# Attention and two gated layers on one core: block 0's softmax divided at its output

## The chip, the cores and the metric

One core of a Trainium2 chip runs the whole program. The metric is device time in microseconds (us). The engines are TensorE (PE in the profile; PEld is its weight load), VectorE (DVE), ScalarE (ACT), GpSimd (POOL) and SyncE (SP), which issues most DMAs.

## The reference

Attention over 2 batches, 8 heads, 768 positions and heads of 64, with a window of 96 positions and 8 global ones, then a SiLU layer (512 to 2048 to 512) and a gated sigmoid layer (512 to 1536 to 512) on the 1536 tokens. All is float32.

```python
def _attn_ref(q, k, v, n_global, n_local):
    scores = scale * np.matmul(q, k.transpose(0, 1, 3, 2))
    ...
    scores = np.where(keep, scores + bias, -1000000000.0)
    scores = scores - np.max(scores, axis=-1, keepdims=True)
    a = np.exp(scores)
    a = a / (np.sum(a, axis=-1, keepdims=True) + 1e-09)
    return np.matmul(a, v)

x = attention output, one row of 512 for each token
h = x @ w_in;  x = (h * sigmoid(h)) @ w_out
out = (sigmoid(x @ w_gate) * (x @ w_val)) @ w_out2
```

## The kernel before

Attention goes by 12 blocks of 128 queries (6 for each batch) and, in a block, by 4 pairs of heads p. One pair's steps: `emit_T` transposes the pair's q and k on TensorE into PSUM (two 128x128 products with an identity), ACT evacuates it for even pairs and DVE for odd ones into tile kt; `emit_QK` gives the scores of the two heads e in two banks; `scores` (in `soft`) adds the mask and takes the row's extreme on DVE (CUSTOM_DVE_ANT_0 in the profile, with a READ_ACCUMULATOR behind it); `exps` takes the exponential on ACT and sums each row with accum_out into ssum; `norm` adds 1e-9 to the sums, takes the reciprocal (128x2) and scales the exponentials, on DVE or POOL; `emit_PT` transposes them, ACT copies them to tile pt; `emit_PV` multiplies with v. After the fourth pair `take` splits the block's output into two parts of the two-part float format of the layers: ACT writes the high part of tile x, DVE the low part. A first block of a batch (i == 0, as block 0 is) has one key tile of 128, others two, so 128x256 scores.

Blocks 0 and 1 are run by `att_units` before anything else; from block 2 on `block_units` weaves the attention into the first layer's products (`macro`), until about 155 us; the rest is the two layers (`phase_rest`, `pair_loops`). Weights are loaded into stage tiles and converted on the way ("splits": one ACT copy to u, on DVE one TENSOR_SCALAR, two SCALAR_TENSOR_TENSOR and one TENSOR_TENSOR that writes w, all 128x512, and one more ACT copy).

Every instruction after `en.begin()` is recorded and then set in order by a planner (`order`), engine by engine, from the costs in `Op.cost` and the dependences that `link` finds. Each engine runs its own list in that order, so an instruction that comes late holds all behind it. In the planner's idle gaps on TensorE in the first blocks it sets filler products of a tile of zeros (warm). All recorded instructions carry one line (L269), so rows are told apart by tiles. In blocks 0 and 1 the transposes of q and k go to two banks in turn (bank 4, bank 6); later both halves of bank 4 are used. In its tail the kernel adds products to acc (`down`) and stores acc from SP.

Of the kernel before, what the change touches and what calls it, by code (L numbers as in the profile page):

```python
# [23 lines left out]
)  # L24
HA = 8
STORES = ((1, 3), (1, 2, 3), (0, 1, 2, 3))
SLOTS = sum(r[-1] for r in PLAN)
SLACK = 0.5
NEG = 1.0e30
# [89 lines left out]
class Issue:  # L119
# [22 lines left out]

    def link(self):
        last = self.last
        for i, o in enumerate(self.ops[self.first:], self.first):
            o.i = i
            for r, w in o.acc:
                if r[1] == bass.MemoryType.DRAM:
                    continue
                keep = []  # L150
                for j, rj, wj in last.get(r[0], ()):
                    hit = j != i and (w or wj) and meets(r, rj)
                    if hit:
                        o.pred.add(j)
                    inside = w and hit and r[2] <= rj[2] and r[3] >= rj[3] and len(r[4]) == 1 and all(
                        r[4][0][0] <= a and b <= r[4][0][1] for a, b in rj[4]
                    )
                    if not inside:
                        keep.append((j, rj, wj))
                keep.append((i, r, w))  # L160
                last[r[0]] = keep
        for o in self.ops[self.first:]:
            for j in o.pred:
                if j >= self.first:
                    o.left += 1
                    self.ops[j].succ.append(o.i)
# [134 lines left out]
def attn_moe_moe2_kernel(  # L301
# [14 lines left out]
    nc = tc.nc  # L316
# [20 lines left out]
    ident = const.tile([128, 128], F32, name="ident")  # L337
    nval = const.tile([128, 4], F32, name="nval")
    flag = const.tile([1, 1], I32, name="flag")
    X = [main.tile([128, 2, KD, G], F32R, name=f"x{g}") for g in range(NG)]  # L340
    acc = [main.tile([128, 4, 512], F32, name=f"acc{g}") for g in range(2)]
    nm_all = main.tile([128, NBLK, H], F32, name="nm_all")
# [26 lines left out]
    def defer(n, fn):  # L369
        seq[0] += 1  # L370
        deferred.append((clock[0] + n, seq[0], fn))
# [58 lines left out]
    def wtile(key):  # L430
        return W[slots[wid[key]]]
# [86 lines left out]
    def need_w(key):  # L518
        n = wid[key]
        while wst["split"] <= n:  # L520
            m = wst["split"]
            if m >= wst["dma"]:
                assert slot_free(m)
                dma_w(m)
                wst["dma"] = m + 1
            assert can_split(m)
            split_w(m)
            wst["split"] = m + 1
# [178 lines left out]
    def soft(n, sp, late=None):  # L707
        if sp is None:
            return
        gi, p = divmod(n, NP)  # L710
        s, i = gi % 2, gi % BLK
        w = 128 if i == 0 else 256
        t = next(t_r)
        t_t[n] = t
        c = 2.0 ** -(2 * p + 1)
        m0 = 0 if i == 0 else (128 if s == 0 else 256)
        ss = ssum[n % 4]

        def scores():
            for e in range(2):  # L720
                en.vector.tensor_tensor_reduce(
                    t[:, e, 0:w], sp[e], mask[e][:, m0:m0 + w], op0=ALU.add, op1=ALU.min,
                    scale=-c, scalar=3.0e38, accum_out=nm_all[:, gi, 2 * p + e:2 * p + e + 1],
                )

        def exps():
            for e in range(2):
                en.scalar.activation(
                    out=t[:, e, 0:w], in_=t[:, e, 0:w], func=AF.Exp, scale=-1.0,
                    bias=nm_all[:, gi, 2 * p + e:2 * p + e + 1], accum_out=ss[:, e:e + 1],  # L730
                )

        def norm():
            en.vector.tensor_scalar(ss, ss, 1.0e-9, None, op0=ALU.add)
            en.vector.reciprocal(ss, ss)
            for e in range(2):
                if n < 2 * NP and e == 0:
                    en.vector.tensor_scalar(t[:, e, 0:w], t[:, e, 0:w], ss[:, e:e + 1], None, op0=ALU.mult)
                else:
                    en.gpsimd.tensor_scalar(  # L740
                        t[:, e, 0:w], t[:, e, 0:w], ss[:, e:e + 1], 1.0, op0=ALU.mult, op1=ALU.mult
                    )

        if late:
            defer(late, scores)
        else:
            scores()
        d = n % 2 if late is None else late
        defer(1 + d, exps)
        defer(2 + d, norm)  # L750

    def emit_PT(n):
        gi, p = divmod(n, NP)
# [16 lines left out]
    def emit_PV(n):  # L770
        gi, p = divmod(n, NP)
        if n < 0 or gi >= NBLK:
            return
        s, i = gi % 2, gi % BLK
        pt = pt_t.pop(n)
        ps = bk["PV"][gi % len(bk["PV"])]
        if i == 0:
            vs = [v_t[gi]]
        else:
            vs = [v_t[gi], v_t[gi - 1]] if s == 0 else [v_t[gi - 1], v_t[gi]]  # L780
        nk = len(vs)
        for c in range(nk):
            for e in range(2):
                en.tensor.matmul(
                    ps[64 * e:64 * e + 64, p * 128:(p + 1) * 128],
                    vs[c][:, (2 * p + e) * D:(2 * p + e + 1) * D],
                    pt[:, (e * nk + c) * 128:(e * nk + c + 1) * 128],
                    start=(c == 0),
                    stop=(c == nk - 1),
                )  # L790

    def take(n):
        gi, p = divmod(n, NP)
        if n < 0 or gi >= NBLK or p < NP - 1:
            return
        i = gi % BLK
        ps = bk["PV"][gi % len(bk["PV"])]
        g, j = divmod(gi, BPG)
        xs = slice(j * 128, (j + 1) * 128)
        pv = ps.rearrange("p (a b) -> p a b", a=NP)  # L800
        en.scalar.activation(out=X[g][:, 0, :, xs], in_=pv, func=AF.Copy)
        en.vector.tensor_tensor(X[g][:, 1, :, xs], pv, X[g][:, 0, :, xs].bitcast(F32), ALU.subtract)
        if 0 < i < BLK - 1:
            en.sync.dma_start(
                out=v_t[gi][0:N_GLOB, :].rearrange("p (h d) -> p h d", h=H),
                in_=v[gi // BLK, :, 0:N_GLOB, :].rearrange("h p d -> p h d"),
            )
        load_v(gi + 2)
# [280 lines left out]
    def pair_loops(accs, evac):  # L1089
# [175 lines left out]

        def down(p, g, gts):
            keys = [("o2", 2 * p + j) for j in range(2)]
            end = p == C2 // 2 - 1
            stored = 0
            for t in range(4):  # L1270
                yb = bank[6 + ny[0] % 2]
                ny[0] += 1
                final = t == 3 and g == NG - 1
                runs = 2 if end and final else 1
                for h in range(runs):
                    cut = slice(h * 512 // runs, (h + 1) * 512 // runs)
                    for j, key in enumerate(keys):
                        need_w(key)
                        mm3_t(yb[:, cut], gts[g, j], slice(t * 128, (t + 1) * 128), wtile(key)[:, :, cut], j == 0, j == 1)
                        if final and h == runs - 1 and j == 1:  # L1280
                            done_w(keys[0])
                            done_w(keys[1])
                        yield unit()
                    a = accs[g][:, t, cut]
                    if p == 0:
                        en.scalar.activation(out=a, in_=yb, func=AF.Copy)
                    else:
                        en.vector.tensor_tensor(a, a, yb[:, cut], ALU.add)
                    if end and t in STORES[g]:
                        r0 = g * G  # L1290
                        en.sync.dma_start(
                            out=out[r0 + stored * 128:r0 + (t + 1) * 128, cut].rearrange("(t p) d -> p t d", p=128),
                            in_=accs[g][:, stored:t + 1, cut],
                        )
                if t in STORES[g]:
                    stored = t + 1

        def mm3_t(ps, gt, cols, w, first, last):
            with en.together():
                for i, (a, b) in enumerate(((0, 0), (0, 1), (1, 0))):  # L1300
                    en.tensor.matmul(ps, gt[:, a, cols], w[:, b, :], start=first and i == 0, stop=last and i == 2)
# [213 lines left out]

    with ExitStack():
        nc.vector.memset(warm, 0.0)
        make_identity(nc, ident)
        en.begin()
        load_qk(0)  # L1520
        make_iota()
        load_qk(1)
        load_v(0)
        load_v(1)
        make_n(qk_t.pop("n"))
        make_mask0()
        bk.update(SA=[bank[0]], SB=[bank[1]], PT=[bank[2], bank[7]], PV=[bank[3]], T=[bank[4], bank[6]])
        emit_T(0)
        emit_T(1)
        make_mask1()  # L1530
# [57 lines left out]
```

## Time and profile before

| | us |
|---|---|
| median of 3 runs | 637.54 (637.10 to 637.62) |
| the profiled execution | 636.38 |
| its span | 634.6 |
| TensorE busy, of the span | 622.5 |
| VectorE busy | 501.8 |
| ScalarE busy | 355.3 |
| GpSimd busy | 79.8 |

The busy times are averages over stages: VectorE's share is 79% of the span, and in the first 80 us far more. The groups below read the stages apart. TensorE's busy time includes modelled ends and fillers.

### The profile page before, as it was taken

How to read it: one execution, taken by the hardware profiler on the slowest of the kernel's cores; microseconds unless marked ns; L12 is line 12 of the kernel's file. 1: busy time of each engine (PE TensorE's matmuls, PEld its weight loads, DVE VectorE, ACT ScalarE, POOL GpSimd, SP SyncE). 2: the span in 40 equal slices, each digit the busy share in tenths (PEclk: the TensorE clock that was granted, in tenths of full speed). 3: DMA queues.
4: the chain of work that ended last, by engine and by line, in shares of the span. 5: the costliest groups of instructions: out<-in, count | busy, mean ns of one | idle time of the engine just before them, and what ended most of it. 6: DMA issues, size and time to landing. Idle time of an engine off the chain costs nothing.

```text
span 634.6 us, 9894 instructions
## 1 busy us (share of the span) xinstructions
PE 622.5 (98%) x3536; PEld 522.6 (82%) x3536; DVE 501.8 (79%) x1138; ACT 355.3 (56%) x751; POOL 79.8 (13%) x167
## 2 busy tenths in 40 slices
PE   8899999999999999999999999999999999999995
PEld 5589877888888888888888898898898898898894
DVE  6999995555379759698979998699789888986553
ACT  5898878655246456364546776754554553552430
POOL 5364445344110000000000000000000000000000
PEclk9899999999999999999999999999999999999999
DMA  8766652200012322222230102321412313200004
GB/s 235 194 163 181 180 135 52 52 19 2 1 34 67 94 72 67 66 68 84 83 100 1 37 31 77 124 66 35 126 40 68 101 33 93 86 22 1 0 35 170
DMA packets 65400, 49.07 MB, mean 77 GB/s; under 512 B 39616, under 2 KB 60352, under 8 KB 65344
## 3 DMA queue, kind: packets, MB, share of 16 engines
q1 hardware_dynamic: 64128, 48.11, 25.9%
q8 instruction: 29, 0.48, 0.3%
q10 hardware_dynamic: 1216, 0.26, 0.2%
q14 instruction: 27, 0.22, 0.1%
HBM read 45.22 MB, written 3.15 MB: 76 GB/s over the span
## 4 chain that ended last, share of the span: by engine, by line


## 5 line engine op out<-in xcount | busy, mean ns | idle before, releaser
L269 PE MATMUL bank<-x,w 128*128 128x512 f32 (+1 forms) x1104 | 238.0, 355 | 0.0
L269 PEld LDWEIGHTS bank<-x,w 128*128 128x128 f32 x1104 | 183.5, 189 | 27.9 <-issue 0.5
L269 PE MATMUL bank<-g,w 128*128 128x512 f32 (+1 forms) x624 | 145.5, 377 | 0.0
L269 PEld LDWEIGHTS bank<-g,w 128*128 128x128 f32 x624 | 110.6, 188 | 21.7 <-issue 0.7
L269 PE MATMUL bank<-w,g 128*128 128x512 f32 (+1 forms) x438 | 105.8, 387 | 0.0
L269 PEld LDWEIGHTS bank<-w,g 128*128 128x128 f32 x438 | 80.9, 188 | 16.7 <-issue 0.3
L269 DVE TENSOR_TENSOR acc<-acc,bank 128x512 f32<-128x512 f32 (+1 forms) x85 | 57.6, 678 | 32.7 <-PE bank L269 32.3
L269 ACT ACTIVATE m<-bank 128x512 f32<-128x512 f32 (+1 forms) x80 | 41.0, 516 | 68.3 <-PE bank L269 66.4
L269 PE MATMUL bank<-t,w 128*128 128x512 f32 x288 | 74.8, 390 | 0.0
L269 PEld LDWEIGHTS bank<-t,w 128*128 128x128 f32 x288 | 53.9, 188 | 11.5 <-ACT m L269 0.4
L269 DVE SCALAR_TENSOR_TENSOR u<-stage,u 128x512 int32<-128x512 int32 x84 | 58.5, 698 | 0.6
L269 DVE TENSOR_TENSOR m<-m,bank 128x512 f32<-128x512 f32 (+1 forms) x72 | 40.8, 574 | 18.3 <-ACT m L269 11.0
L269 ACT ACTIVATE w<-u 128x512 fp32r<-128x512 f32 x62 | 38.9, 627 | 26.6 <-DVE u L269 23.4
L269 ACT ACTIVATE t<-t,nm_all 128x256 f32<-128x256 f32 (+1 forms) x96 | 46.0, 481 | 9.9 <-DVE nm_all L269 9.4
L269 ACT ACTIVATE sg<-bank 128x512 f32<-128x512 f32 (+1 forms) x52 | 28.5, 548 | 39.5 <-PE bank L269 38.3
L269 POOL TENSOR_SCALAR t<-t,ssum 128x256 f32<-128x256 f32 (+1 forms) x88 | 44.8, 525 | 30.7 <-DVE ssum L269 17.8
L269 DVE TENSOR_TENSOR w<-u,w 128x512 fp32r<-128x512 f32 x62 | 43.2, 697 | 3.0 <-ACT w L269 2.7
L269 DVE SCALAR_TENSOR_TENSOR acc<-bank,acc 128x512 f32<-128x512 f32 x48 | 32.6, 689 | 10.0 <-PE bank L269 9.6
L269 DVE CUSTOM_DVE_ANT_0 t<-bank,mask 128x256 f32<-128x256 f32 (+1 forms) x96 | 34.7, 394 | 4.1 <-PE bank L269 2.7
L269 ACT ACTIVATE g<-sg 128x512 fp32r<-128x512 f32 x40 | 25.2, 630 | 21.8 <-DVE sg L269 12.5
L269 DVE SCALAR_TENSOR_TENSOR stage<-stage,stage 128x512 int32<-128x512 int32 x52 | 35.8, 688 | 0.2
L269 DVE TENSOR_TENSOR g<-m,g 128x512 fp32r<-128x512 f32 x44 | 30.0, 689 | 7.0 <-ACT g L269 6.6
(109 smaller groups left out, 718.7 us busy)
## 6 DMA issues: line engine op xcount, KB each, us to landing
stage<-in_moe_w_out_dram SPq DMA_DIRECT2D x28, 512.0 KB, 3.8
stage<-in_moe_w_in_dram SPq DMA_DIRECT2D x16, 512.0 KB, 3.8
stage<-in_moe_w_gate_dram SPq DMA_DIRECT2D x12, 512.0 KB, 3.4
stage<-in_moe_w_val_dram SPq DMA_DIRECT2D x12, 512.0 KB, 3.4
v<-in_v_dram SPq DMA_DIRECT2D x12, 256.0 KB, 2.9
qk<-in_k_dram SPq DMA_DIRECT2D x11, 256.0 KB, 3.1
qk<-in_q_dram SPq DMA_DIRECT2D x11, 256.0 KB, 4.1
out_dram<-acc SPq DMA_DIRECT2D x3, 512.0 KB, 2.7
```

The costliest lines, as they stand in the source:

```text
L269: getattr(getattr(self.nc, o.eng), o.meth)(*o.args, **o.kw)
```

## The change

For block 0 alone (LATE_SUMS = 1) the exponentials stay undivided and lose accum_out, and `norm` is left out. Behind the products with v the same transposed exponentials are multiplied with a tile of ones into a bank of their own, SUM (bank 6), so that each output row has its sum beside it. In `take` VectorE adds 1e-9 to that bank (128x512), takes the reciprocal of 128x512 and multiplies the block's output with it into tile sg, from which the high and low parts are then made. Since bank 6 holds the sums, the transposes of blocks 0 and 1 use the two halves of bank 4. Block 0's v is loaded ahead of block 1's k and q. `link` gains a rule that one accumulation in a bank may not start before the one before it in that bank has stopped. In the tail each 128-row tile of the output is stored by itself, and the last one is made and stored whole, not in two halves of columns.

```diff
-STORES = ((1, 3), (1, 2, 3), (0, 1, 2, 3))
+LATE_SUMS = 1
...
     def link(self):
...
+            if o.form == "f":
+                b = o.outs[0].name
+                if o.kw["start"] and b in ended:
+                    o.pred.add(ended[b])
+                if o.kw["stop"]:
+                    ended[b] = i
...
         def exps():
             for e in range(2):
+                sums = {} if gi < LATE_SUMS else {"accum_out": ss[:, e:e + 1]}
                 en.scalar.activation(
                     out=t[:, e, 0:w], in_=t[:, e, 0:w], func=AF.Exp, scale=-1.0,
-                    bias=nm_all[:, gi, 2 * p + e:2 * p + e + 1], accum_out=ss[:, e:e + 1],
+                    bias=nm_all[:, gi, 2 * p + e:2 * p + e + 1], **sums,
                 )
...
-        defer(2 + d, norm)
+        if gi >= LATE_SUMS:
+            defer(2 + d, norm)
...
     def emit_PV(n):
...
+        if gi >= LATE_SUMS:
+            return
+        for c in range(nk):
+            for e in range(2):
+                en.tensor.matmul(
+                    bk["SUM"][64 * e:64 * e + 64, p * 128:(p + 1) * 128],
+                    ones.to_broadcast([128, 64]), pt[:, (e * nk + c) * 128:(e * nk + c + 1) * 128],
+                    start=(c == 0),
+                    stop=(c == nk - 1),
+                )
...
     def take(n):
...
+        if gi < LATE_SUMS:
+            r, q1 = next(u_r), next(e_r)
+            en.vector.tensor_scalar(r, bk["SUM"], 1.0e-9, None, op0=ALU.add)
+            en.vector.reciprocal(r, r)
+            en.vector.tensor_tensor(q1, ps, r, ALU.mult)
+            pv = q1.rearrange("p (a b) -> p a b", a=NP)
...
         def down(p, g, gts):
...
-                final = t == 3 and g == NG - 1
-                runs = 2 if end and final else 1
...
+                if p == C2 // 2 - 1:
+                    r0 = g * G + t * 128
+                    en.sync.dma_start(out=out[r0:r0 + 128, :], in_=a)
...
         nc.vector.memset(warm, 0.0)
+        nc.vector.memset(ones, 1.0)
...
+        load_v(0)
         load_qk(1)
-        load_v(0)
         load_v(1)
...
-        bk.update(SA=[bank[0]], SB=[bank[1]], PT=[bank[2], bank[7]], PV=[bank[3]], T=[bank[4], bank[6]])
+        bk.update(SA=[bank[0]], SB=[bank[1]], PT=[bank[2], bank[7]], PV=[bank[3]],
+                  T=[bank[4][:, 0:256], bank[4][:, 256:512]], SUM=bank[6])
```

VectorE's list in block 0 before, from the scores of pairs 0 and 1 in their second head (ISA, tiles t) on; ssum are the sums, kt an evacuation of transposed q and k:

```order
L269 ISA t_136,nm_all<-bank_65,mask_114 128x128
L269 ISA nm_all 128x1
L269 ISA t_137,nm_all<-bank_65,mask_114 128x128
L269 ISA nm_all 128x1
L269 TENSOR_SCALAR ssum_123<-ssum_123 128x2
L269 RECIPROCAL ssum_123<-ssum_123 128x2
L269 TENSOR_SCALAR t_136<-t_136,ssum_123 128x128
L269 TENSOR_SCALAR ssum_124<-ssum_124 128x2
L269 ISA t_133,nm_all<-bank_64,mask_113 128x128
L269 ISA nm_all 128x1
L269 RECIPROCAL ssum_124<-ssum_124 128x2
L269 ISA t_133,nm_all<-bank_65,mask_114 128x128
```

The same place of VectorE's list after the change:

```order
L276 ISA t_137,nm_all<-bank_65,mask_115 128x128
L276 ISA nm_all 128x1
L276 ISA t_138,nm_all<-bank_65,mask_115 128x128
L276 ISA nm_all 128x1
L276 TENSOR_SCALAR kt_117<-bank_68 128x256
L276 ISA t_134,nm_all<-bank_64,mask_114 128x128
L276 ISA nm_all 128x1
L276 ISA t_134,nm_all<-bank_65,mask_115 128x128
L276 ISA nm_all 128x1
L276 ISA t_135,nm_all<-bank_64,mask_114 128x128
L276 ISA nm_all 128x1
L276 ISA t_135,nm_all<-bank_65,mask_115 128x128
```

The small instructions on ssum and the scaling of t are gone between the scores of block 0, and an evacuation of block 1 (kt) has moved in.

VectorE's list at the end of block 1 before, from the last part of the first weight split (w) on; x is the low part of block 0's output, u a split of the second weight:

```order
L269 TENSOR_TENSOR w_83<-u_102,w_83 128x512
L269 TENSOR_SCALAR t_136<-t_136,ssum_124 128x256
L269 TENSOR_TENSOR x_75<-bank_67,x_75 128x4x128
L269 ISA t_133,nm_all<-bank_65,mask_114 128x256
L269 ISA nm_all 128x1
L269 TENSOR_SCALAR ssum_125<-ssum_125 128x2
L269 TENSOR_SCALAR u_103<-u_103 128x512
L269 RECIPROCAL ssum_125<-ssum_125 128x2
L269 SCALAR_TENSOR_TENSOR u_103<-stage_100,u_103 128x512
L269 TENSOR_SCALAR ssum_126<-ssum_126 128x2
L269 TENSOR_SCALAR kt_116<-bank_70 128x2x128
L269 TENSOR_SCALAR t_137<-t_137,ssum_125 128x256
```

The same place after the change, where bank_70 is the bank of sums, bank_67 block 0's output and sg the divided output:

```order
L276 TENSOR_TENSOR w_84<-u_103,w_84 128x512
L276 TENSOR_SCALAR t_137<-t_137,ssum_125 128x256
L276 TENSOR_SCALAR u_104<-bank_70 128x512
L276 ISA t_134,nm_all<-bank_64,mask_114 128x256
L276 ISA nm_all 128x1
L276 RECIPROCAL u_104<-u_104 128x512
L276 TENSOR_SCALAR ssum_126<-ssum_126 128x2
L276 TENSOR_TENSOR sg_109<-bank_67,u_104 128x512
L276 RECIPROCAL ssum_126<-ssum_126 128x2
L276 TENSOR_SCALAR ssum_127<-ssum_127 128x2
L276 TENSOR_SCALAR t_138<-t_138,ssum_126 128x256
L276 RECIPROCAL ssum_127<-ssum_127 128x2
```

The three wide instructions of the division stand ahead of the scalings (t) of block 1's last two pairs; the work on the second weight (u from a stage tile) has moved behind.

SP's list at the start before, with k and q of block 1 in qk_129 and v of block 0 in v_130:

```order
L269 DMA qk_128<-in_k_dram 128x4x64
L269 DMA qk_129<-in_k_dram 128x8x64
L269 DMA qk_129<-in_q_dram 128x8x64
L269 DMA v_130<-in_v_dram 128x8x64
L269 DMA v_131<-in_v_dram 128x8x64
```

The same place after, where they are qk_130 and v_131:

```order
L276 DMA qk_129<-in_k_dram 128x4x64
L276 DMA v_131<-in_v_dram 128x8x64
L276 DMA qk_130<-in_k_dram 128x8x64
L276 DMA qk_130<-in_q_dram 128x8x64
L276 DMA v_132<-in_v_dram 128x8x64
```

Block 1's k and q each stand one transfer of 256 KB later. From about the 330th of some 1,900 rows of TensorE on, all lists are the same as before up to the last tile.

## Rows read from the trace of the kernel before

**Rows 1.** Busy time by stage: length, then each engine's, granted clock, DMA share, GB/s

```profile
8.50:13.80 5.30, 4.78 (x34) 2.89 (x33) 4.40 (x29) 4.63 (x21) 2.18 (x9) 1.00 1.04 334
13.80:26.40 12.60, 10.23 (x74) 7.03 (x75) 12.40 (x46) 11.53 (x32) 4.12 (x9) 0.92 0.86 212
26.40:80.00 53.60, 52.65 (x489) 46.83 (x489) 51.54 (x164) 46.76 (x125) 27.43 (x51) 0.99 0.62 173
80.00:155.00 75.00, 74.53 (x552) 60.03 (x547) 48.20 (x194) 52.62 (x155) 35.42 (x72) 1.00 0.23 55
155.00:628.00 473.00, 473.00 (x2351) 400.60 (x2349) 379.99 (x686) 237.56 (x419) 5.14 (x4) 1.00 0.20 62
```

**Rows 2.** Timeline of VectorE in block 0: start, us, operation, count, idle before

```profile
5.28 0.42 DVE L269 TENSOR_SCALAR kt<-bank 128x256 f32<-128x256 f32 x1 [0.60 <-PE bank L269]
...
8.51 0.29 DVE L269 CUSTOM_DVE_ANT_0 t<-bank,mask 128x128 f32<-128x128 f32 x1
...
10.46 0.17 DVE L269 TENSOR_SCALAR ssum<-ssum 128x2 f32<-128x2 f32 x1 [0.35 <-ACT t L269]
10.66 0.17 DVE L269 RECIPROCAL ssum<-ssum 128x2 f32<-128x2 f32 x1
10.86 0.29 DVE L269 TENSOR_SCALAR t<-t,ssum 128x128 f32<-128x128 f32 x1
11.07 0.16 DVE L269 TENSOR_SCALAR ssum<-ssum 128x2 f32<-128x2 f32 x1
...
13.82 0.43 DVE L269 CUSTOM_DVE_ANT_0 t<-bank,mask 128x256 f32<-128x256 f32 x1 [0.24 <-PE bank L269]
```

**Rows 3.** Issues of DMA at 3.53 and 3.94 us: median us to landing last

```profile
qk<-in_k_dram SPq DMA_DIRECT2D x1, 256.0 KB, 3.4
qk<-in_q_dram SPq DMA_DIRECT2D x1, 256.0 KB, 3.9
```

**Rows 4.** VectorE by shape, whole span: count, busy us, mean ns, idle before

```profile
L269 DVE TENSOR_TENSOR x<-bank,x 128x512 fp32r<-128x512 f32 x12 | 8.2, 686 | 1.6 <-ACT x L269 1.6
L269 DVE COPY acc<-bank 128x512 f32<-128x512 f32 x8 | 5.5, 683 | 4.1 <-PE bank L269 4.1
```

**Rows 5.** Three single short instructions of VectorE, at 4.33, 10.46 and 10.66 us

```profile
L269 DVE TENSOR_SCALAR nval<-nval 128x1 f32<-128x1 f32 x1 | 0.2, 154 | 0.0
...
L269 DVE TENSOR_SCALAR ssum<-ssum 128x2 f32<-128x2 f32 x1 | 0.2, 170 | 0.3 <-ACT t L269 0.3
...
L269 DVE RECIPROCAL ssum<-ssum 128x2 f32<-128x2 f32 x1 | 0.2, 167 | 0.0
```

**Rows 6.** Timeline of VectorE from block 0's x to block 2's first scores

```profile
19.55 0.69 DVE L269 TENSOR_TENSOR x<-bank,x 128x512 fp32r<-128x512 f32 x1
20.15 0.42 DVE L269 CUSTOM_DVE_ANT_0 t<-bank,mask 128x256 f32<-128x256 f32 x1
...
24.61 0.69 DVE L269 TENSOR_TENSOR w<-u,w 128x512 fp32r<-128x512 f32 x1
25.21 0.68 DVE L269 SCALAR_TENSOR_TENSOR u<-stage,u 128x512 int32<-128x512 int32 x1
26.03 0.43 DVE L269 TENSOR_SCALAR u<-u 128x512 int32<-128x512 int32 x1
26.38 0.42 DVE L269 CUSTOM_DVE_ANT_0 t<-bank,mask 128x256 f32<-128x256 f32 x1
```

**Rows 7.** Timeline of TensorE: block 0's products with v, block 2's scores

```profile
13.98 0.66 PE L269 MATMUL bank<-pt,v 128*64 128x128 f32 x8
14.57 0.39 PE L1512 MATMUL bank<-warm 128*128 128x256 bf16 x2
...
23.68 0.66 PE L269 MATMUL bank<-ident,t 128*128 128x128 f32 x4 [0.60 <-DVE t L269]
24.27 3.67 PE L269 MATMUL bank<-kt 64*128 64x256 f32 x16
...
36.50 2.00 PE L269 MATMUL bank<-kt 64*128 64x256 f32 x16
```

**Rows 8.** The tail: last adds and stores, stores by size with us to landing

```profile
628.26 0.75 DVE L269 TENSOR_TENSOR acc<-acc,bank 128x256 f32<-128x256 f32 x2 [0.74 <-PE bank L269]
...
628.71 0.99 SPq L269 DMA_DIRECT2D out_dram<-acc  x2
...
out_dram<-acc SPq DMA_DIRECT2D x5, 256.0 KB, 2.0
out_dram<-acc SPq DMA_DIRECT2D x2, 128.0 KB, 2.0
```

More of the change, by code (lines that the diff above doesn't have):

```diff
@@ L144, in link @@
         last = self.last
+        ended = {}
         for i, o in enumerate(self.ops[self.first:], self.first):
             o.i = i
+            if o.form == "f":
[4 more added lines that the diff above has]
+                    ended[b] = i
             for r, w in o.acc:
@@ L339, in attn_moe_moe2_kernel @@
     flag = const.tile([1, 1], I32, name="flag")
+    ones = const.tile([128, 1], F32, name="ones")
     X = [main.tile([128, 2, KD, G], F32R, name=f"x{g}") for g in range(NG)]
@@ L1267, in down @@
             keys = [("o2", 2 * p + j) for j in range(2)]
-            end = p == C2 // 2 - 1
-            stored = 0
             for t in range(4):
@@ L1272, in down @@
                 ny[0] += 1
-                final = t == 3 and g == NG - 1
-                runs = 2 if end and final else 1
[L1275 to L1296, printed above, removed]
+                for j, key in enumerate(keys):
+                    need_w(key)
+                    mm3_t(yb, gts[g, j], slice(t * 128, (t + 1) * 128), wtile(key), j == 0, j == 1)
+                    if t == 3 and j == 1 and g == NG - 1:
+                        done_w(keys[0])
+                        done_w(keys[1])
+                    yield unit()
+                a = accs[g][:, t, :]
+                if p == 0:
+                    en.scalar.activation(out=a, in_=yb, func=AF.Copy)
+                else:
+                    en.vector.tensor_tensor(a, a, yb, ALU.add)
+                if p == C2 // 2 - 1:
+                    r0 = g * G + t * 128
+                    en.sync.dma_start(out=out[r0:r0 + 128, :], in_=a)
         def mm3_t(ps, gt, cols, w, first, last):
```

## Prediction

> **What bounds the kernel now.** I read the stages first, because the shares of the whole span mix them [rows 1]. From 155 us on TensorE is busy for all of 473.00 us: what the kernel is late there, it is late at the end, and nothing is made up. From 80 to 155 TensorE has 0.47 us of idle and VectorE is busy for only 48.20 of 75. Before 80 us it is the other way: from 13.80 to 26.40 VectorE is busy for 12.40 of 12.60 us while TensorE has 2.4 us of idle, and from 26.40 to 80 VectorE is busy for 51.54 of 53.60 us. The change stands in the first 25 us, so the engine to count is VectorE. TensorE's waits there say the same: at 23.68 it waited 0.60 us for VectorE's scaled t [rows 7]. Then I read VectorE's timeline [rows 2, 6] and the prices of its forms [rows 4, 5], and last the tail [rows 8].
>
> The profiled execution took 636.38 us, 1.16 less than the median of the runs, 637.54. I make the sum against 636.38 and add the 1.16.
>
> **Part 1: what block 0 loses.** VectorE drops twelve instructions: for each of four pairs an add and a reciprocal of 128x2 and a scaling of 128x128. Short ones overlap, so I count from start to start: the first pair's are 0.20 (10.46 to 10.66), 0.20 and 0.21 us [rows 2]. Ten of the twelve stand ahead of block 1's first scores and by this count take 1.8 us, the other two 0.28 us. Two waits go with them: 0.35 us for the sum at 10.46, and 0.60 us at 5.28, since the evacuation kt now stands behind four mask instructions. If all of that and the wait of 0.24 us ahead of 13.82 came through, block 1's first scores would start 3.0 us earlier; that is one bound, no gain the other.
>
> I take half of it, 1.5 us, since new waits are late next. Transposes that went to two banks now go to the halves of one, and the lists let the evacuations of it follow one another, so that block 1's last kt waits for ACT's before it. And v stands ahead of block 1's k and q on SP's queue: those two landed 3.4 us after 3.53 and 3.9 after 3.94, at 6.9 and 7.8, so 256 KB cost 0.9 us and q now lands at about 8.8 [rows 3]. Block 1's transposes start with it. That v itself comes earlier gives nothing: block 0's products with v ran at 13.98 without a wait for it [rows 7]. So block 1's first scores: 13.82 - 1.5 = 12.3 us.
>
> ACT loses the accumulator reads of eight exponentials and POOL four scalings, both off VectorE's path. TensorE gains eight products with ones; the eight with v took 0.66 us, and fillers stand right behind them at 14.57 [rows 7], so they take the place of fillers and cost nothing; if they did not, 0.66 us. The memset of ones precedes VectorE's first wait and costs nothing.
>
> **Part 2: what the division costs.** Three instructions of 128x512 are added to VectorE, ahead of the scalings of block 1's last two pairs, which TensorE's transposes wait for, and so ahead of block 2's scores. The add and the product read PSUM as the rows of 683 and 686 ns do [rows 4]; queued, such a one takes 0.60 us from start to start (19.55 to 20.15, [rows 6]), so 1.2 us for both.
>
> The reciprocal of 128x512 is not in the trace. The nearest row by shape, 0.69 us [rows 4], is the lower bound; queued, 0.60. The same operation on 128x2 took 167 ns, and the shortest row with one source, on 128x1, took 154 [rows 5]. If the 13 ns between them are the cost of two elements, one costs 6.5 ns, and 512 cost 3.3, with the fixed 0.15 some 3.5 us. If they are the cost of the one element more, 512 cost 6.7 and the whole 6.8 us, the upper bound. Against both stands that a TENSOR_SCALAR on 128x2 took 170 ns, more than the reciprocal [rows 5]. I take 3.5 us, from the row of the operation itself.
>
> The Trainium skill (VectorE: DVE Perf Modes, "First, the fixed hardware budget") says that the reciprocal is an iterative divide with a repeat count of 8. Read as 8 cycles an element at that page's 0.96 GHz it would be an estimate of 4.4 us, and the sum below 0.9 us higher; the row's 6.5 ns agrees in direction and is some six such cycles.
>
> **Part 3: the account at block 2.** From block 1's first scores to block 2's, 13.82 to 26.38, there are 12.56 us, of which VectorE idles about 0.2 [rows 1, 2, 6]. Of it go 0.28 us of part 1 and come 1.2 + 3.5 = 4.7 us. The new list also puts off weight splits behind block 2's first scores: the 128x512 instructions at 24.61, 25.21 and 26.03 and one more, together about 2.1 us. So block 2's scores start at 12.3 + 12.56 - 0.28 + 4.7 - 2.1 = 27.2 us, 0.8 later than now, and VectorE owes 2.1 us more. In work done it is 2.9 us behind, 2.7 if the 0.2 of idle is used.
>
> **Part 4: what arrives at the end.** From 26.40 to 80 us VectorE has 2.06 us of idle, waits for engines that stand behind it in the same chain; TensorE has 0.95 [rows 1]. I let half of TensorE's idle be used up and carry 2.2 to 2.3 us to 155 us, from where all of it stays.
>
> The clock of TensorE: block 2's sixteen score products took 3.67 us against 2.00 for the next block's [rows 7], at a granted clock of 0.92 in the mean of that stage [rows 1]. TensorE had waited for VectorE before. It will wait again, so I give this the same price; 1.7 us either way if not.
>
> **Part 5: the tail.** The last tile was added in two halves of 0.75 us together, both after the last product, and stored by two issues of 0.99 us, the second some 0.6 after the first at 628.71 [rows 8]. Whole, it takes one add of 0.69 us, and twelve products become six, 0.08 us shorter; the single store issues at about 628.9 instead of 629.3. A store of 256 KB landed in 2.0 us like one of 128 KB [rows 8], so 0.4 us are gained (bounds 0 to 0.5). The stores ahead of it are hidden behind products.
>
> **Sum:** 636.38 + 2.3 - 0.4 = 638.3, and with 1.16 about 639.4 us.
>
> **Rivals.**
> A. The reciprocal costs no more than any 128x512 instruction, 0.60 queued, as the 170 ns of rows 5 would have it. Then 2.9 us fall out of the account: 2.7 - 2.9 - 0.4 = -0.6, 637.0 us, not slower.
> B. The reciprocal costs 3.5 us but the owed splits are absorbed in VectorE's later idle, since TensorE is the engine that is full from 26.4 on (52.65 of 53.60, [rows 1]). Then the path from scores to scores alone counts: +0.8 - 0.4, 637.9 us. Against it: VectorE's 2.06 us of idle would have to be used nearly whole.
> C. Both: a cheap reciprocal, and only that path counts. Block 2's scores start 2.1 us earlier than now (0.8 - 2.9): -2.1 - 0.4, 635.0 us.
> D. The reciprocal is at its upper bound: 3.3 us more than forecast, 642.7 us.
> That the change does not do what it says: block 0's v ahead gains nothing, as worked out above.
>
> **Chances.** Forecast 0.46, A 0.19, B 0.20, C 0.10, D 0.05. For the price of the reciprocal I go by the 13 ns at 7 in 10. A measurement of this kernel tells 0.2%, some 1.3 us, from no change. Faster needs under 636.3, slower over 638.8. The forecast's own range is 638.2 to 640.6, so four fifths of it count as slower; A is same in seven of ten cases, B nearly always; C is mostly faster. That gives faster 0.16, same 0.39, slower 0.45. The range from 635.7 to 641.0 leaves out most of C, D and the forecast's upper end.
>
> **What would show it.** In the profile after: one RECIPROCAL of 128x512 with 3 to 4 us on VectorE near 19 us; block 1's first scores of 128x256 near 12.3 us; block 2's sixteen score products on TensorE between 24 and 26 us, and its first scores near 27 us; TensorE idle behind that reciprocal, waiting for t; TensorE full from 155 us on, shifted by 2 us; a last store that issues 0.4 us sooner after the last product. A RECIPROCAL of 0.7 us makes the forecast wrong at once and leaves A or C. One of 3.5 us with an end that is the same means B, and then the stretch from 26 to 80 us must hold less idle than the 2.06 us now.

## The result

The change makes the kernel slower. In runs that alternate on one chip it takes 640.57 us (median of 6, 639.61 to 641.47) where the kernel before takes 637.36 (6 runs, 636.44 to 637.72): a ratio of 1.0051, 95% interval 1.0038 to 1.0063, which is 3.3 us (2.4 to 4.0). The forecast was 639.4 us, 1.9 over the median that it started from; the time lies in its range, at the upper end of the forecast's own (638.2 to 640.6). The profiled execution of the kernel after took 641.03 us with a span of 639.2, that of before 636.38 with 634.6, so the two traces lie 4.6 us apart, more than the medians. That of before ended 1.0 us under the median above and that of after 0.5 over its own. Part of this is the start: of the executions profiled here, that of before is one of those whose TensorE started early (below).

The stages of the kernel after, which answer to [rows 1] (length; busy time and count of PE, PEld, DVE, ACT and POOL; granted clock; DMA share; GB/s):

```profile
8.50:13.80 5.30, 5.22 (x42) 3.83 (x44) 3.90 (x23) 3.74 (x13) 1.94 (x8) 1.00 1.15 311
13.80:26.40 12.60, 8.92 (x79) 6.94 (x76) 12.55 (x38) 9.54 (x29) 2.88 (x7) 0.90 0.73 163
26.40:80.00 53.60, 51.80 (x458) 45.34 (x457) 51.05 (x164) 45.33 (x121) 26.16 (x49) 0.96 0.66 174
80.00:155.00 75.00, 73.94 (x563) 59.66 (x563) 49.78 (x197) 54.07 (x157) 34.56 (x71) 1.00 0.28 65
155.00:628.00 473.00, 473.00 (x2350) 400.51 (x2349) 379.15 (x689) 239.52 (x423) 8.29 (x9) 1.00 0.19 60
```

VectorE lost 0.5 us of work in block 0's stage, is as full as before up to 26.40 us, and does other work there: 38 instructions instead of 46 in the same time. From 155 us on TensorE is full in both, so nothing of the lateness is made up.

VectorE's timeline of the kernel after, against [rows 2] and [rows 6] (start, us, operation, idle before it and what ended that):

```profile
7.50 0.42 DVE L276 TENSOR_SCALAR kt<-bank 128x256 f32<-128x256 f32 x1 [1.74 <-PE bank L276]
...
9.62 0.28 DVE L276 CUSTOM_DVE_ANT_0 t<-bank,mask 128x128 f32<-128x128 f32 x1
...
12.71 0.42 DVE L276 TENSOR_SCALAR kt<-bank 128x256 f32<-128x256 f32 x1 [0.37 <-ACT t L276]
13.80 0.42 DVE L276 CUSTOM_DVE_ANT_0 t<-bank,mask 128x256 f32<-128x256 f32 x1 [0.67 <-PE bank L276]
...
19.27 0.68 DVE L276 TENSOR_SCALAR u<-bank 128x512 f32<-128x512 f32 x1
19.87 0.41 DVE L276 CUSTOM_DVE_ANT_0 t<-bank,mask 128x256 f32<-128x256 f32 x1
...
20.21 3.35 DVE L276 RECIPROCAL u<-u 128x512 f32<-128x512 f32 x1
23.48 0.10 DVE L276 TENSOR_SCALAR ssum<-ssum 128x2 f32<-128x2 f32 x1
23.59 0.69 DVE L276 TENSOR_TENSOR sg<-bank,u 128x512 f32<-128x512 f32 x1
24.20 0.15 DVE L276 RECIPROCAL ssum<-ssum 128x2 f32<-128x2 f32 x1
...
27.33 0.42 DVE L276 TENSOR_SCALAR kt<-bank 128x256 f32<-128x256 f32 x1 [0.83 <-PE bank L276]
...
29.23 0.42 DVE L276 CUSTOM_DVE_ANT_0 t<-bank,mask 128x256 f32<-128x256 f32 x1
```

The reciprocal of 128x512 takes 3.35 us, 3.27 from its start to the next one's. Block 1's first scores come at 13.80, where before they came at 13.82: what the twelve dropped instructions gave is gone by then, above all in the wait of 1.74 us ahead of the first kt, up to 0.8 of which is the late start of this execution (below). Block 2's first scores come at 29.23 instead of 26.38.

TensorE in the kernel after, against [rows 7]:

```profile
0.97 4.66 PE L1527 MATMUL bank<-warm 128*128 128x256 bf16 x21 [0.97 <-DVE ones L1533]
5.43 0.63 PE L276 MATMUL bank<-ident,qk 128*128 128x128 f32 x2
...
24.80 1.97 PE L276 MATMUL bank<-ident,t 128*128 128x128 f32 x8 [2.69 <-DVE t L276]
26.56 0.63 PE L276 MATMUL bank<-ident,qk 128*128 128x128 f32 x2
27.12 3.72 PE L276 MATMUL bank<-kt 64*128 64x256 f32 x16
```

It idles 2.69 us behind the reciprocal, and the eight transposes after it take 1.97 us and block 2's score products 3.72. In before the first two rows read so:

```profile
0.97 3.83 PE L1512 MATMUL bank<-warm 128*128 128x256 bf16 x21 [0.97 <-DVE warm L1517]
4.64 0.60 PE L269 MATMUL bank<-ident,qk 128*128 128x128 f32 x4
```

The same 21 warm products took 0.83 us longer in the execution of after, and TensorE's first real product came 0.79 us later. In other executions shown here that product came anywhere from 4.61 to 5.43 us, in kernels of both kinds. With the very lists of before it came at 4.64, 5.32 and 5.43 us (before, e9_vswap, e10_onelist). So up to 0.8 us of what separates the two traces is this, and no part of the change. It does not always arrive: e9_vswap starts 0.68 us late, its block 2's scores are 0.66 late, and the first product of its layers only 0.13.

### The profile page after: what moved, and what is told of

Its sections match the earlier page's. It is cut to its first block, busy times and chain, and to the rows that moved or that the text cites. A ratio compares the mean times of both kernels' runs of the same rounds, so it can differ in the third digit from the quotient of the medians.

```text
span 639.2 us, 9900 instructions
## 1 busy us (share of the span) xinstructions
PE 625.4 (98%) x3546; PEld 525.4 (82%) x3546; DVE 503.1 (79%) x1129; ACT 354.2 (55%) x743; POOL 78.8 (12%) x163
## 4 chain that ended last, share of the span: by engine, by line
PE 90%; DVE 8%; issue 1%; ACT 0%; POOL 0%; DVEq 0%
PE bank L276 89%; DVE u L276 3%; DVE t L276 2%; DVE w L276 1%; PE bank L1527 1%; DVE x L276 1%; DVE acc L276 1%; DVE ssum L276 0%; DVE kt L276 0%; DVE sg L276 0%; POOL t L276 0%; ACT x L276 0%; DVE nm_all L276 0%; DVE mask L276 0%; ACT sg L276 0%
## 5 line engine op out<-in xcount | busy, mean ns | idle before, releaser
L276 PE MATMUL bank<-w,g 128*128 128x512 f32 x432 | 105.7, 390 | 0.0
L276 DVE TENSOR_TENSOR acc<-acc,bank 128x512 f32<-128x512 f32 x84 | 57.4, 683 | 32.4 <-PE bank L276 32.0
L276 POOL TENSOR_SCALAR t<-t,ssum 128x256 f32<-128x256 f32 (+1 forms) x84 | 43.1, 530 | 34.2 <-DVE ssum L276 27.1
```

The source lines that it names most:

```text
L276: getattr(getattr(self.nc, o.eng), o.meth)(*o.args, **o.kw)
```

## Experiments

Three theories went in. V: VectorE is the engine to count up to 80 us, so its added work arrives at the end. C: TensorE's idle time behind the reciprocal and the low clock after it cost a second time. B: the shared bank for the transposes eats what the dropped instructions gave. Two more came up on the way: Q, that v ahead of k and q on SP's queue costs by itself, and L, that a small edit costs through the new lists that the planner makes from it. In e1_mult and e2_hold every engine's list is that of after, in e9_vswap, e10_onelist and e12_dose that of before, but for the edit itself; e3_tail differs from before in its last tile alone. In the others the planner made new lists.

All times beside the ratios are from the traces: TensorE's first transposes of q and k, the first scores of blocks 1 and 2 on VectorE, and the first and the 151st product of the first layer (bank<-x,w) on TensorE, all in us from the span's start.

| kernel | first transposes | block 1 | block 2 | first x,w | 151st x,w | ratio to before, 95% |
|---|---|---|---|---|---|---|
| before | 4.64 | 13.82 | 26.38 | 31.46 | 122.65 | |
| after | 5.43 | 13.80 | 29.23 | 34.36 | 127.76 | 1.0051 (1.0038 to 1.0063) |
| e1_mult | 5.43 | 13.66 | 25.75 | 30.20 | 123.70 | 1.0007 (0.9999 to 1.0016) |
| e2_hold | 5.27 | 13.36 | 28.10 | 32.70 | 127.23 | 1.0058 (1.0045 to 1.0071) |
| e3_tail | 4.81 | 13.83 | 26.37 | 31.42 | 122.82 | 1.0000 (0.9991 to 1.0008) |
| e4_onebank | 5.23 | 14.54 | 28.84 | 33.30 | 125.59 | 1.0051 (1.0037 to 1.0065) |
| e5_ptbank | 4.61 | 14.51 | 30.54 | 35.20 | 128.61 | 1.0091 (1.0076 to 1.0106) |
| e6_late | 5.43 | 13.77 | 32.25 | 37.14 | 129.81 | 1.0059 (1.0046 to 1.0073) |
| e7_vfirst | 5.43 | 14.57 | 28.24 | 32.78 | 129.92 | 1.0075 (1.0056 to 1.0093) |
| e8_ptlate | 5.37 | 14.46 | 33.28 | 38.85 | 129.90 | 1.0103 (1.0088 to 1.0118) |
| e9_vswap | 5.32 | 14.46 | 27.04 | 31.59 | 122.92 | 1.0006 (0.9997 to 1.0016) |
| e10_onelist | 5.43 | 16.29 | 29.40 | 33.99 | 125.71 | 1.0041 (1.0027 to 1.0054) |
| e11_noV | 4.83 | 15.40 | 31.46 | 36.02 | 128.01 | 1.0072 (1.0058 to 1.0086) |
| e12_dose | 5.43 | 14.64 | 30.86 | 36.36 | 127.47 | 1.0069 (1.0055 to 1.0082) |

**The reciprocal taken out of the kernel after (e1_mult).**

```diff
-            en.vector.reciprocal(r, r)
+            en.vector.tensor_tensor(r, r, r, ALU.mult)
```

> The kernel after, with the wide reciprocal of block 0 replaced by a product of the same shape (so block 0's outputs are not divided but multiplied by their sums); every engine's list is otherwise the same as after. Theory V (VectorE's account): the 3.35 us of the reciprocal, queued some 3.3, become about 0.6 and the 2.7 us between go through to the end: about 637.9 us where after takes 640.6, and block 2's first scores come 2.7 us earlier, at 26.5. Theory C (TensorE's low clock behind the reciprocal costs a second time): the idle of 2.69 us at 24.80 goes, the sixteen score products fall from 3.72 towards 2.0, and up to 1.7 us more are gained, 636.2. Theory O (what is lost lies in the order of the lists, not in the reciprocal): no more than 1 us is gained, 639.6 or more.

It took 636.99 us where before took 636.77: from a ratio of 1.0051 to one of 1.0007, 2.8 us, with the two intervals some 1.0 either way. VectorE's timeline at the same place:

```profile
20.07 0.68 DVE L276 TENSOR_TENSOR u<-u 128x512 f32<-128x512 f32 x1
20.68 0.16 DVE L276 TENSOR_SCALAR ssum<-ssum 128x2 f32<-128x2 f32 x1
...
25.75 0.41 DVE L276 CUSTOM_DVE_ANT_0 t<-bank,mask 128x256 f32<-128x256 f32 x1
```

A product of the same shape costs 0.61 us from start to start, so 2.66 us of VectorE's time went. V's 637.9, C's 636.2 and O's 639.6 were said beside 637.4 for before, so 0.5 over it, 1.2 under it and 2.2 over it. Measured is 0.4 over it (-0.1 to 1.0): V fits, and C and O are out. The trace alone would not part V from C, since block 2's scores come 3.5 us earlier than in after where V said 2.7, and the sixteen score products take 2.00 us here too. With a product in the reciprocal's place the rest of the change is worth nothing: the same as before within what can be measured.

**The clock held up (e2_hold).**

```diff
+        if n == 6:
+            en.ops[-2 * nk].hold = 24
...
+                    for _ in range(o.hold):
+                        filler()
```

> The kernel after, with 24 warm products put on TensorE ahead of the transposes that wait behind the reciprocal, some 2.6 us of work in the 2.69 us that it idles there. Theory C: the granted clock stays up, block 2's sixteen score products take about 2.0 us instead of 3.72, and 1.7 us go off the end: 638.9. Theory V: VectorE sets the pace, block 2's first scores come at most 1 us earlier, and the end stays within 0.4 us of after, 640.2 to 640.8.

TensorE's timeline:

```profile
21.50 2.78 PE L1531 MATMUL bank<-warm 128*128 128x256 bf16 x24
24.35 1.27 PE L278 MATMUL bank<-ident,t 128*128 128x128 f32 x8
25.65 0.44 PE L278 MATMUL bank<-ident,qk 128*128 128x128 f32 x2
26.01 2.00 PE L278 MATMUL bank<-kt 64*128 64x256 f32 x16
```

The edit did what it should: the score products took 2.00 us and the transposes 1.27. Block 2's first scores came at 28.10, 1.1 us before those of after, of which 0.16 is the start. At the 151st product 0.5 of it is left, and the time shows none: 1.0058 against 1.0051, as V said. But the low clock was only moved. Further on TensorE waited for GpSimd's scaled t, and the layers' first six products behind that wait took 1.63 us, where in after they took 0.96:

```profile
31.35 0.89 PE L278 MATMUL bank<-ident,t 128*128 128x128 f32 x4 [1.44 <-POOL t L278]
...
32.70 1.63 PE L278 MATMUL bank<-x,w 128*128 128x256 f32 x6
```

So C falls as a cost that can be saved at this place: TensorE came earlier, and then waited. What the low clock costs if it stays away altogether is not shown.

**The tail alone (e3_tail).** The kernel before with `down` as it is after:

```diff
-                final = t == 3 and g == NG - 1
-                runs = 2 if end and final else 1
...
+                if p == C2 // 2 - 1:
+                    r0 = g * G + t * 128
+                    en.sync.dma_start(out=out[r0:r0 + 128, :], in_=a)
```

> The kernel before with the tail alone changed: the last tile is computed whole and stored by one issue, and each tile of the last pair has its own store. If the tail gives what the sum says, 0.4 us less than before (bounds 0 to 0.5), 637.0 where before takes 637.4, with all that precedes the last products unchanged. If the more numerous stores get into each other's way, no gain or a loss of up to 0.3.

The time is the same, -0.6 to +0.5 us. In the trace the products stand 0.2 us later than in before and the span is 0.4 shorter (634.2 for 634.6), so the tail gives some 0.5 us, as the rows said; it is less than can be timed. The tail of the kernel after, against [rows 8]:

```profile
633.27 0.69 DVE L276 TENSOR_TENSOR acc<-acc,bank 128x512 f32<-128x512 f32 x1 [0.67 <-PE bank L276]
633.98 0.36 SPq L276 DMA_DIRECT2D out_dram<-acc  x1
```

**The shared bank alone (e4_onebank), and again with the lists of before (e10_onelist).**

```diff
-        bk.update(SA=[bank[0]], ..., T=[bank[4], bank[6]])
+        bk.update(SA=[bank[0]], ..., T=[bank[4][:, 0:256], bank[4][:, 256:512]])
```

> The kernel before with the transposes of q and k of blocks 0 and 1 in the two halves of one bank instead of two banks, and nothing else of the change. Theory B (the shared bank eats the start): VectorE's evacuation kt of the second pair waits for the third pair's transposes, block 0's first scores come at about 9.6 instead of 8.51, block 1's about 1 us later than 13.82, and the end is 0.8 to 1.5 us later, about 638.5. Rival S (the start lost its gain only through TensorE's slow clock in that one execution): block 0's first scores within 0.3 us of 8.5 and the end as before, 637.4.

It cost 3.2 us (2.4 to 4.1), as much as the whole change. S, which had the end as before, is out. VectorE waits for the next pair's transposes as B said, but block 0's first scores come at 9.05 us, which is no later than in before once the later start (0.6) is taken off, and block 1's first scores only 0.1 us later; 1.7 us more are lost between them and block 2's scores, where VectorE now has eight instructions on stage tiles instead of six, in a list that is not that of before. So the bank and the list had to be told apart. In e10_onelist the recorded instructions carry the old bank numbers for the planner and the new ones for the chip:

```diff
+        if ALIAS:
+            a, b = ALIAS
...
+                self.banks = {b if x == a else x for x in self.banks}
```

> The kernel before with its lists as they were, and the transposes of q and k of blocks 0 and 1 in the halves of one bank, the planner still counting them as two banks. Theory B (the bank itself): each evacuation kt waits for the next pair's transposes and these for the evacuation before, in lists that don't allow for it, so block 1's first scores come 1 us or more later and the end 1 to 3 us, 638.2 to 640.2. Theory L (the planner's new lists cost the 0.5% that sharing the bank cost): within 0.8 us of before, 637.2 to 638.0.

In this kernel block 2's fourth pair of transposes is written over the second pair's before that is read, so block 2 has wrong keys there; the instructions, their number and their order are the same. VectorE's timelines, of e4_onebank and then of e10_onelist:

```profile
6.96 0.42 DVE L269 TENSOR_SCALAR kt<-bank 128x256 f32<-128x256 f32 x1 [1.25 <-PE bank L269]
```

```profile
7.04 0.42 DVE L276 TENSOR_SCALAR kt<-bank 128x256 f32<-128x256 f32 x1 [2.41 <-PE bank L276]
...
11.47 0.42 DVE L276 TENSOR_SCALAR kt<-bank 128x256 f32<-128x256 f32 x1 [0.73 <-PE bank L276]
...
16.29 0.42 DVE L276 CUSTOM_DVE_ANT_0 t<-bank,mask 128x256 f32<-128x256 f32 x1 [0.24 <-PE bank L276]
```

With unchanged lists the bank costs 2.6 us (1.7 to 3.4): B holds. The delay is there when the first layer starts (2.5 us, 0.8 of them the start) and stays (3.1 at the 151st product).

**Two banks again in the kernel after (e5_ptbank).**

```diff
-        PT=[bank[2], bank[7]], ..., T=[bank[4][:, 0:256], bank[4][:, 256:512]],
+        PT=[bank[2]], ..., T=[bank[4], bank[7]],
```

> The kernel after, with the transposes of q and k of blocks 0 and 1 in two banks again; the second bank is taken from the transposes of the exponentials (PT), which then have one. Theory B (the shared bank eats what the dropped instructions gave): block 0's first scores come at about 8.5 us instead of 9.62, block 1's at 12.3 to 12.8 instead of 13.80, and the end gains between those 1.1 us and the 3.2 that sharing the bank cost the kernel before: 637.2 to 639.3 where after takes about 640.2. Rival P: one bank for PT costs as much, since each pair's transposes wait for the copy of the pair before; block 1's first scores stay at 13.5 or later and the end stays within 0.5 us of after.

```profile
5.30 0.42 DVE L276 TENSOR_SCALAR kt<-bank 128x256 f32<-128x256 f32 x1 [0.57 <-PE bank L276]
...
11.70 0.29 DVE L276 CUSTOM_DVE_ANT_0 t<-bank,mask 128x128 f32<-128x128 f32 x1 [0.97 <-PE bank L276]
...
14.16 0.43 DVE L276 TENSOR_SCALAR u<-u 128x512 int32<-128x512 int32 x1 [1.20 <-ACT u L276]
14.51 0.42 DVE L276 CUSTOM_DVE_ANT_0 t<-bank,mask 128x256 f32<-128x256 f32 x1
```

The first half came true, in an execution that started as early as that of before: the wait of 1.74 us fell to 0.57, and block 0's first scores came at 8.55. The second did not: VectorE now waits 0.97 and 1.20 us further on, and block 1's scores come at 14.51. It took 642.41 us, by the ratios 2.5 more than after. Rival P was nearer in its numbers, and the loss is greater than it said. But its reason, the one bank for PT, is not what the trace shows first. TensorE's list has transposes of block 1 ahead of block 0's last scores, and they waited for block 1's q, which stands behind v:

```profile
9.71 0.55 PE L276 MATMUL bank<-ident,qk 128*128 128x128 f32 x3 [0.83 <-DMA qk<-in_q_dram]
```

VectorE's wait of 0.97 us goes back to that one; for a copy of pt TensorE waits 0.28 us, at 12.75. So this run does not tell what two banks would give. With k and q ahead of v again they were not tried.

**The reciprocal at another place (e6_late), and both edits (e8_ptlate).**

```diff
+            if self.meth == "reciprocal":
+                self.occ = 0.07 + n * 0.0064
...
+            en.slack = 5.0
             en.vector.reciprocal(r, r)
+            en.slack = 0.0
```

> The kernel after, with the planner told what the wide reciprocal takes and holding it back 5 us, so that on VectorE it stands behind block 1's last scalings and block 2's evacuations (kt) instead of ahead of them; no instruction is added or dropped. Theory V (VectorE's account): the 3.3 us are still spent before 80 us, so only the idle comes back that VectorE had behind it (0.83 us at 27.33) and a part of TensorE's slow products; the end is 0 to 1.0 us earlier than after, 639.2 to 640.2. Theory K (only the chain from block 1's scalings to block 2's scores counts): the reciprocal is off that chain, TensorE does not idle 2.69 us at 24.80, and 2.5 us or more are gained, 637.7 or less.

The planner's own cost for the reciprocal had been 0.07 + 512/960 = 0.60 us. VectorE, then TensorE:

```profile
24.19 0.42 DVE L278 TENSOR_SCALAR kt<-bank 128x256 f32<-128x256 f32 x1
24.52 3.34 DVE L278 RECIPROCAL u<-u 128x512 f32<-128x512 f32 x1
```

```profile
28.80 1.11 PE L278 MATMUL bank<-ident,t 128*128 128x128 f32 x4 [4.81 <-DVE sg L278]
29.84 3.79 PE L278 MATMUL bank<-kt 64*128 64x256 f32 x16
```

No gain that can be measured: 1.0059. But it doesn't decide between V and K, since the reciprocal did not leave the chain: the last pair's transposes go to the bank of block 0's output, which stays occupied until sg is made, so TensorE waited 4.81 us for sg instead of 2.69 for t.

> Both edits at once: the transposes of q and k in two banks, and the reciprocal held back behind block 1's last scalings. Theory V with B: the gains add, 1.1 to 3.2 for the banks and 0 to 1.0 for the place, so 636.0 to 639.1 where after takes about 640.2; it beats the kernel before (about 637) only if both come out near their upper ends. Theory K: 635 or less.

643.67 us, a ratio of 1.0103: neither theory came out, and the loss is about that of e5_ptbank.

**v ahead of k and q, alone (e7_vfirst), with the lists of before (e9_vswap), and taken back in the kernel after (e11_noV).**

```diff
         make_iota()
-        load_qk(1)
         load_v(0)
+        load_qk(1)
```

> The kernel before with block 0's v asked for ahead of block 1's k and q, and nothing else. Theory Q (the queue): q of block 1 lands some 0.9 us later, block 1's transposes of q and k start that much later, VectorE idles for part of it ahead of block 1's scores, and the end is 0.3 to 0.9 us later than before. Rival N: the planner fills the gap with other work and the end is within 0.2 us of before. In neither does the earlier v gain anything, since block 0's products with v never waited for it.

4.8 us (3.6 to 5.9), far outside both. Block 1's scores and the first product of the layers come 0.8 and 1.3 us later than in before, 0.8 of either the start; the rest of the loss comes behind, where VectorE, full in before, is busy for only 48.23 us from 26.40 to 80:

```profile
26.40:80.00 53.60, 49.68 (x444) 45.23 (x441) 48.23 (x158) 44.45 (x120) 24.74 (x48) 0.94 0.59 162
```

The lateness is 1.3 us at the first product of the layers and 5.5 at the 31st, at 47.98 us. Between them the granted clock falls: it is 0.80, 0.86, 1.00 and 0.66 in the four stretches of 5 us from 30 to 50, where before has 1.00 in all four, and TensorE waits 1.54 us for GpSimd's t at 31.52 and 1.33 for its g at 45.00. That speaks for the list, not for the queue, and e9_vswap shows it: the three rows are exchanged on SP's list after planning, and all else stays.

```diff
+            sp = [i for i, o in enumerate(done) if isinstance(o, Op) and o.eng == "sync"]
+            a, b, c = sp[SWAP:SWAP + 3]
+            done[a], done[b], done[c] = done[c], done[a], done[b]
```

> The kernel before with every engine's list as it was, except that on SP's list v of block 0 stands ahead of k and q of block 1 (the three rows are exchanged after planning). Theory Q (the queue itself): q of block 1 lands 0.9 us later, and what the edit cost when the planner could answer it, 0.75% or 4.8 us, is seen again, or at least the 0.9 us carried to the end: 638 to 642. Theory L (the planner's new lists cost it): no more than 0.9 us, 637.2 to 638.1 where before takes 637.2.

0.4 us (-0.2 to 1.0). L holds: the queue costs little, and some 4 us of e7_vfirst were the planner's answer to it. TensorE waits for q until 9.05 us instead of 7.90, and block 1's scores are not late by it (0.64 us, with 0.68 of the start). In this execution block 2's score products ran at the higher clock, behind the same waits of TensorE as in before:

```profile
24.91 2.00 PE L274 MATMUL bank<-kt 64*128 64x256 f32 x16
...
30.32 0.89 PE L274 MATMUL bank<-ident,t 128*128 128x128 f32 x4 [1.52 <-POOL t L274]
```

Of the 1.67 us that this saves, TensorE spends 1.52 waiting for GpSimd's t. The lateness is 0.66 us at block 2's scores, 0.43 at its next transposes and 0.13 at the first product of the layers.

> The kernel after with block 1's k and q asked for ahead of block 0's v again. Theory Q: what that order cost the kernel before, 0.9 to 4.8 us, comes back: 635.4 to 639.3 where after takes 640.4, and at the lower end it beats the kernel before. Theory L: the planner makes other lists again, and the end moves by no more than 1 us either way, 639.4 to 641.4.

Its edit is the reverse of e7_vfirst's, in the kernel after. 640.94 us, 1.0072: nothing came back, as L said, and block 1's scores came at 15.40. Here too the lists are others; it does not beat before.

**A dose of VectorE (e12_dose).**

```diff
+        nc.vector.memset(dummy, 1.0)
...
+        if gi == 0:
+            en.ops[-1].hook = lambda: nc.vector.reciprocal(dummy, dummy)
```

> The kernel before with its lists as they were, and one reciprocal of 128x512 more on VectorE, of a tile that nothing else uses then, just ahead of block 0's low part x at 19.55 us (and a memset of that tile where VectorE idles at the start). No planner answers it. Theory V: 3.27 us, the time from start to start behind the wide reciprocal in after, less the 0.2 us that VectorE idles in that stage, and all of it stays: 640.2 where before takes 637.2. Rival I (absorbed in VectorE's 2.06 us of idle from 26.4 to 80): 1.0 to 1.5 us, 638.2 to 638.7.

```profile
20.36 3.35 DVE L807 RECIPROCAL sg<-sg 128x512 f32<-128x512 f32 x1
23.63 0.63 DVE L271 TENSOR_TENSOR x<-bank,x 128x512 fp32r<-128x512 f32 x1
...
30.86 0.42 DVE L271 CUSTOM_DVE_ANT_0 t<-bank,mask 128x256 f32<-128x256 f32 x1 [0.25 <-PE bank L271]
```

4.4 us (3.5 to 5.2) where V said 3.0 and the rival 1.0 to 1.5: more than either. In the trace x is 4.08 us later than in before: 0.8 of the start and 3.27 of the reciprocal. At block 2's scores it is 4.5, 0.25 of the difference a wait for TensorE; at the first product of the layers it is 4.9, and at the 151st 4.8. With the lists held fixed, a reciprocal on VectorE at 20 us arrives at the end whole and none of it is absorbed: that much of V is shown, and the rival is out. That some 1 us more arrives (0.2 to 1.9), V had not said. It may be TensorE's low clock, since behind an idle time of 3.79 us eight transposes took 2.37 us, where in before two groups of four took 0.66 each; that it is the whole of it is not shown.

```profile
26.45 2.37 PE L271 MATMUL bank<-ident,t 128*128 128x128 f32 x8 [0.40 <-DVE t L271]
```

## Why the prediction was right, and where it was not

The sign and the cause were right: the reciprocal's price, VectorE as the engine that counts, and lateness that stays. The sum was too small by 1.4 us (1.9 forecast, 3.3 measured over before), and its larger errors lie on one side.

**Part 1** is the step that failed. It gave block 1's first scores 1.5 us; the trace shows 0.0, and with the 0.8 us of the late start taken off about 0.8. It named the last kt as the late one. The one that waited was the first, 1.74 us ahead of 7.50, for the next pair's transposes, which wait for the evacuation before. The wait is the shared bank's: e5_ptbank, with two banks, has 0.57 there, and e10_onelist, with the lists of before and one bank, 2.41, where before has 0.60; of the 1.74 and the 2.41 some 0.8 is the late start of those two executions. The two halves of a bank don't overlap, and still the program's semaphores hold the engines apart. The Trainium skill (PSUM — Partial Sum Buffer, "PSUM bank collisions raise a hardware error") asks for just that: semaphores by bank, or by bank and quadrant, and not by address, since two engines in one bank and quadrant collide even at other columns. The runs agree as far as the wait goes; what happens without it none of them shows.

**Part 2** was right: 3.35 us for 3.5 forecast, and 0.60 and 0.61 for the add and the product. Of the two readings of [rows 5], 13 ns for two elements was the good one: from 128x2 (0.17 us) to 128x512 it is 6.2 ns an element, though the 170 ns of a 128x2 TENSOR_SCALAR had spoken against it. The estimate of 4.4 us from the Trainium skill's repeat count (VectorE: DVE Perf Modes, "First, the fixed hardware budget") is a third too high here; the measurement decides.

**Part 3** put block 2's scores 14.9 us behind block 1's; it was 15.43. The 0.5 us are the wait of 0.83 at 27.33 for TensorE, whose eight transposes took 1.97 us at the low clock and 1.27 in e2_hold, where the distance is 14.74. The owed weight splits were put at 2.1 us: from block 2's scores to the 151st product the lateness grows from 2.85 to 5.11. In e1_mult it grows by 1.7, from -0.63 to 1.05 us, without the reciprocal. In e12_dose, which has the reciprocal and the lists of before, it goes from 4.5 to 4.8. In time, the lists of before and after differ until about 99 us of the trace of before. So most of this part belongs to the list and not to the division, and rival B, which let it be absorbed, is out.

**Part 4** let 0.4 to 0.7 us be absorbed before 155 us; nothing was. That the clock would have the same price was right for the score products (3.72 for 3.67), and e2_hold shows that giving it back at that place moves the end by no more than can be measured.

**Part 5** was right in the trace (some 0.5 us for 0.4), and v's place, put at 0.9 us of q's landing, makes TensorE wait for q 1.15 us longer in e9_vswap and is worth 0.4 us (-0.2 to 1.0) there.

By the traces, the lateness at block 2's scores is 2.85 us for 0.8 forecast: 0.8 of the start, 0.7 that part 1 lacks, and 0.55 of part 3. The traces overstate the end: their spans lie 4.6 us apart and the medians 3.2. The parts do not add up singly: one bank 3.2, v first 4.8 and the reciprocal 2.8 make 10.8 us, and all together cost 3.3. The first two were re-planned, and e7_vfirst beside e9_vswap shows that a new list can cost several times what its edit does (4.8 and 0.4 us). What remains open: which rows of e7_vfirst's list, most of them between 31 and 48 us, lose the 4 us; what a planner that knows the reciprocal's price would do without holding it back; and what the twelve dropped instructions would give with two banks for each step. For that there is a bank that was not tried: in blocks 0 and 1 bank 5 takes nothing but the filler products.

## What to carry to other kernels

Before a division is moved to where it costs fewer instructions, count its elements: a reciprocal of two columns four times is 0.7 us, one of 512 columns 3.35, and here 64 rows of each half hold the same sums. Where a planner orders the work, an edit's own price is read only with the lists held fixed; the re-planned kernel mixes it with the price of another list. And a bank that is given to a new step has to be paid for by the step that loses it, here with 2.6 us (e10_onelist).

## What the runs showed of the hardware

TensorE's pace at the start differs from execution to execution, with the same list too (4.64 us to the first real product in before, 5.43 in e10_onelist). From 4 to 5 us the stage rows of before and of after (columns as above) count 12 products and 7, both fully busy:

```profile
4.00:5.00 1.00, 1.00 (x12) 0.94 (x10) 0.61 (x4) 0.01 (x1) 0.61 (x1) 1.00 1.12 253
```

```profile
4.00:5.00 1.00, 1.00 (x7) 0.69 (x5) 0.90 (x5) 0.01 (x1) 0.59 (x1) 1.00 1.18 231
```

Warm products start every 0.213 us at first; in before this becomes 0.109 behind the 15th, and in after it holds for all 21. By that pace before was at the higher of TensorE's two levels (2.4 GHz) and after still at the lower (1.2 GHz), with warm products alone ahead in both; the column of the granted clock reads 1.00 in both rows, so this rise is read from the products and not from it. It moved TensorE's first real product by up to 0.8 us. Waits of the same length were followed by either level: behind 0.59, 0.40 and 0.60 us block 2's score products took 3.67 us in before and 2.00 in e9_vswap. And 24 warm products in an idle gap of 2.69 us kept the higher level: the sixteen score products behind them took 2.00 us, and 3.72 where the gap stayed open.
